# Fourier mixing and a squared-ReLU layer on one core: angle tables built by other engines in another order, weights loaded later, one small permutation of the second block moved

## The chip, the core and the metric

The kernel runs on one core of a Trainium2 chip. The core has a matrix engine (TensorE, PE in the profile; its weight loads are PEld), a vector engine (VectorE, DVE), a scalar engine (ScalarE, ACT), a general engine (GpSimd, POOL) and a synchronisation engine (SyncE, SP). Each works through its own list of instructions in order, and they meet only at semaphores. On-chip memory is SBUF, with 128 partitions; matrix products land in PSUM. POOL here also issues nearly all loads. A load issued by POOL occupies POOL while its descriptors are made, and is carried out by 16 DMA engines later.

The metric is device time in microseconds (us). Before the change it is 598.44 us, the median of three runs (597.36 to 598.6).

## The reference

`x` has shape (8, 3008, 256), `w_in` (256, 2048), `w_out` (2048, 256), all float32.

```python
X = np.fft.fft(x, axis=1)
X = np.fft.fft(X, axis=2)
x = X.real.reshape(B * S, D)
h = np.maximum(x @ w_in, 0.0)
return h * h @ w_out
```

## The kernel before

The 2-D transform's real part is written as cosine and sine products. The cosine and sine matrix over the 256 features is multiplied into `w_in` first, which gives `gh` (three float16 matrices of 128 rows and 2048 columns). The transform over 3008 rows is folded several times by symmetry, so that TensorE multiplies folded rows `od` by tables `cos_t` and `sin_t` of 376 columns. Results of all eight blocks (batches) are laid side by side in one long line of columns, which is cut into windows of 240, 512, 376, 376, 512, 448 and then 512 columns. For each window TensorE multiplies `gh` by the window's `zc` and `zs` (lines 859, 860, 882), ScalarE applies ReLU, VectorE squares (`power`, line 898), and one window later TensorE multiplies by `wout16` (line 704). The order of the work is written out by hand (`tc.manual_schedule()`): the order of the Python calls is the order on each engine.

What follows concerns the time before the first window and the second window (`w == 1`).

**Loads.** POOL issues, in this order, a direct load of half of the first block `x` (line 127), two gathers of the other half (line 132), two loads for `w16` (line 180, `w_in`), one for `wout16` (line 329), and later three loads of the second block. Loads of one queue land in their order of issue.

**Tables.** `table_steps(0)` makes the tables in two halves of three rows (h = 0, 1). The angle is frequency times row number, reduced modulo the period. `args` (ACT, line 232, three instructions for each half) makes `t`, a rounded number of turns; `turns` (line 238) scales it, on DVE for half 0 and on POOL for half 1; `mods(0)` (DVE, line 254, three instructions) multiplies the frequency `kf` by the row `nvec` and adds `t`. For half 1 the same is done in two steps: `kns(1)` (ACT, line 244, three instructions) makes the product `m`, `sums(1)` (DVE, line 248, one instruction of 1128 elements) adds `t`. `sins` (ACT, line 260) turns `m` into `sin_t`. `weigh` (POOL, line 281) halves one row of `sin_t` on one partition, with a weight `wgt` that POOL makes (lines 322, 323). `coss` (lines 270, 271) makes two rows of `cos_t` at a time: two TensorE products with a permutation matrix (`perm`, POOL, line 326) turn rows of `sin_t` over, and ACT copies them out of PSUM. The second `coss` reads the weighed row.

`s_n` and `c_all` (ACT, lines 315, 317, 331) are the feature tables, from `am` and `at` on DVE.

**First fold.** `u_half` and `u_odd` (DVE, lines 396, 400) subtract quarters of the first block, `u_part(0)` (lines 403, 370) gives `od`; a copy of one row (line 397) lies between the first two. `edge` (ACT, line 407) sets column 0 of `od`.

**TensorE's list before window 0.** 44 products on zeros (`idle`, line 307), `coss(0)`, 4 more on zeros, `coss(1)`, `coss(2)`, 5 more, then the first three products with `od` (line 581, `pz`), then `gh_step(0)`: four products of `c_all` and `s_n` with `w16` (line 527), then `nyq` (lines 453 to 455: two small products of `perm` with column d = 128 of `od`, and a DVE copy of the result into column 0 of the sine half of `od`), more of line 581, `gh_step(1)`, then the first products of window 0 (line 938). `gh_turn` (DVE, line 534) needs `turn2`, which POOL makes after its loads (lines 337, 338). After `gh_turn(1)` DVE adds the quarters of block zero (`v_even`, line 410), which frees `x` for the load of block one.

**Window 1** goes by pairs of steps, p = 0 to 3. In each, TensorE makes `pq(s0)` and `pq(s1)` (four products each), ACT applies ReLU to both. DVE folds block one meanwhile (lines 431, 442, 435, 445, and 448, which writes `od`). For p = 3 the calls are

```python
pq(s0); relu(s0, 0); pq(s1); relu(s1, 0)
run(*post[s0 - 1])          # nyq of block one
settle(); power(s1, 0, 1)   # the squares that wait
run(*zl)                    # 12 products pz with od
```

and at the end of p = 2 one square is taken out of turn: `kept.pop(0)()`.

Of the kernel before, what the change touches and what calls it, by code (L numbers as in the profile page):

```python
# [10 lines left out]
F16 = mybir.dt.float16  # L11
# [5 lines left out]
P = 128  # L17
# [12 lines left out]
def kernel(  # L30
# [145 lines left out]
    xs = {0: load_x(0, idx_first)}  # L176
    prow_i = iota([P, P], [[1, P]], 0, 1, "prow_i")
    w16 = [wp.tile([P, 2, F // 2], F16, name=f"w16_{i}", tag="w16") for i in range(2)]
    for i in range(2):
        nc.gpsimd.dma_start(out=w16[i], in_=moe_w_in[:, i * F // 2 : (i + 1) * F // 2].rearrange("(c p) f -> p c f", p=P))  # L180
# [26 lines left out]
    def table_steps(e):  # L207

        n = unit_cols[e][0]
        nr = 2 if e else 3  # L210
        cos_t = const.tile([P, 2 if e else R, n], F16, name=f"cos{e}")
        sin_t = const.tile([P, 2 if e else R, n], F16, name=f"sin{e}")
        tabs[e] = (cos_t, sin_t)
        vec, vs = (evec, evs) if e else (nvec, nvs)
        st = {}

        def row(h, j):
            return j if e else RQ[3 * h + j]

        def freq():  # L220
            kf = st["kf"] = tmp.tile([P, NE], F32, name="kf", tag="kf")[:, 0:n]
            i = 0
            for k0, kstep, cnt in unit_runs[e][0]:
                nc.vector.tensor_scalar(out=kf[:, i : i + cnt], in0=irow[:, i : i + cnt], scalar1=float(kstep), scalar2=float(k0 - kstep * i), op0=ALU.mult, op1=ALU.add)
                i += cnt

        def args(h):
            t = st["t", h] = tmp.tile([P, 3 * NE], F32, name="t", tag="tt").rearrange("p (j n) -> p j n", j=3)
            for j in range(nr):
                r = row(h, j)  # L230
                if e == 0:
                    nc.scalar.activation(t[:, j, 0:n], st["kf"], AF.Copy, bias=R23, scale=vs[:, r : r + 1])
                else:
                    nc.vector.tensor_scalar(out=t[:, j, 0:n], in0=st["kf"], scalar1=vs[:, r : r + 1], scalar2=R23, op0=ALU.mult, op1=ALU.add)

        def turns(h, eng=nc.vector):
            t = st["t", h]
            eng.tensor_scalar(out=t[:, 0:nr, 0:n], in0=t[:, 0:nr, 0:n], scalar1=-R23, scalar2=-float(S), op0=ALU.add, op1=ALU.mult)

        def kns(h):  # L240
            m = st["m", h] = tmp.tile([P, 3, NE], F32, name="m", tag="tm")
            for j in range(nr):
                r = row(h, j)
                nc.scalar.activation(m[:, j, 0:n], st["kf"], AF.Copy, bias=0.0, scale=vec[:, r : r + 1])

        def sums(h):
            m = st["m", h][:, 0:nr, 0:n]
            nc.vector.tensor_tensor(m, m, st["t", h][:, 0:nr, 0:n], op=ALU.add)

        def mods(h):  # L250
            m = st["m", h] = tmp.tile([P, 3, NE], F32, name="m", tag="tm")
            for j in range(nr):
                r = row(h, j)
                nc.vector.scalar_tensor_tensor(out=m[:, j, 0:n], in0=st["kf"], scalar=vec[:, r : r + 1], in1=st["t", h][:, j, 0:n], op0=ALU.mult, op1=ALU.add)

        def absm(h):
            nc.vector.tensor_scalar(out=st["t", h][:, 0:nr, 0:n].bitcast(I32), in0=st["m", h][:, 0:nr, 0:n].bitcast(I32), scalar1=0x7FFFFFFF, scalar2=None, op0=ALU.bitwise_and)

        def sins(h):
            nc.scalar.activation(sin_t[:, 3 * h : 3 * h + nr, :], st["m", h][:, 0:nr, 0:n], AF.Sin, bias=0.0, scale=wk)  # L260

        def coss(h):
            if e:
                nc.scalar.activation(cos_t, st["t", h][:, 0:nr, 0:n], AF.Sin, bias=halfpi[:, 0:1], scale=-wk)
                return

            pc = ps_h.tile([P, 2, 512], F32, name="pc", tag="psh")
            for j in range(2):
                r = RQ[2 * h + j]
                nc.tensor.matmul(pc[:, j, 0:n], perm[1 if r else 0], sin_t[:, RQ.index(6 - r if r else 0), :], start=True, stop=True)  # L270
            nc.scalar.activation(cos_t[:, 2 * h : 2 * h + 2, :], pc[:, :, 0:n], AF.Copy, bias=0.0, scale=1.0)

        def weigh():
            if e:
                for t in (cos_t, sin_t):
                    for r in range(2):
                        nc.vector.tensor_scalar(out=t[:, r, :], in0=t[:, r, :], scalar1=wge[:, r : r + 1], scalar2=None, op0=ALU.mult)
                return

            q = RQ.index(1)  # L280
            nc.gpsimd.tensor_scalar(out=sin_t[:, q, :], in0=sin_t[:, q, :], scalar1=wgt[:, 0:1], scalar2=1.0, op0=ALU.mult, op1=ALU.mult)
# [24 lines left out]
        for i in range(n):  # L306
            nc.tensor.matmul(pw[:, 0 : 3 * P], spn[:, 0, 0, :], spn.rearrange("p c r d -> p (c r d)")[:, 0 : 3 * P], start=True, stop=True)
# [16 lines left out]
    perm = [const.tile([P, P], F16, name=f"perm{i}") for i in range(2)]  # L324
    for i in (1, 0):
        nc.gpsimd.tensor_scalar(out=perm[i], in0=prow_i, scalar1=float(P - 1 - i), scalar2=None, op0=ALU.is_equal)
    to["sums"](1)

    nc.gpsimd.dma_start(out=wout16, in_=moe_w_out.rearrange("(c p) o -> p c o", p=P))
# [3 lines left out]
    pick = const.tile([P, 1], F16, name="pick")  # L333
    nc.gpsimd.memset(pick, 0.0)
    nc.gpsimd.memset(pick[0:1, :], -2.0)
    turn2 = small([P, 1], "turn2")
    nc.gpsimd.tensor_scalar(out=turn2, in0=dvec[:, 0:1], scalar1=0.0, scalar2=2.0, op0=ALU.is_equal, op1=ALU.mult)
    nc.gpsimd.tensor_scalar(out=turn2, in0=turn2, scalar1=-2.0, scalar2=None, op0=ALU.add)
    evec_i = iota([P, 2], [[1, 2]], 0, 2, "evec_i")
    idx["c"] = iota([P, 1], [[1, 1]], P - 1, -1, "idx_c")  # L340
    nc.gpsimd.memset(idx["c"][0:2, :], P - 3)
    idx["f"] = iota([P, 1], [[1, 1]], -1, 1, "idx_f")
    nc.gpsimd.memset(idx["f"][0:1, :], 0)
    evec = small([P, 2], "evec")
    nc.gpsimd.tensor_copy(evec, evec_i)
    evs = small([P, 2], "evs")
    nc.gpsimd.tensor_scalar(out=evs, in0=evec, scalar1=1.0 / S, scalar2=None, op0=ALU.mult)
    wge = small([P, 2], "wge")
    wg2 = small([P, 2], "wg2")
    nc.gpsimd.tensor_scalar(out=wge, in0=evec, scalar1=float(G), scalar2=0.5, op0=ALU.is_le, op1=ALU.mult)  # L350
    nc.gpsimd.tensor_scalar(out=wg2, in0=evec, scalar1=float(G), scalar2=0.5, op0=ALU.is_lt, op1=ALU.mult)
    nc.gpsimd.tensor_tensor(wge, wge, wg2, op=ALU.add)
    nc.gpsimd.tensor_scalar(out=wg2, in0=evec, scalar1=0.0, scalar2=-0.5, op0=ALU.is_equal, op1=ALU.mult)
    nc.gpsimd.tensor_tensor(wge, wge, wg2, op=ALU.add)
    to["sins"](1)
    folded = {}

    fe = fo = None
# [462 lines left out]
    for w in range(NW):  # L821
# [141 lines left out]
        elif w == 1:  # L963
            zl = [j for zu, part, h in zj for j in zu(part, h)]
            for p in range(NST // 2):
# [97 lines left out]
```

## Time and profile before

| what | us |
|---|---|
| median of three runs | 598.44 |
| the profiled execution's own time | 597.31 |
| its span, first to last instruction | 595.5 |
| TensorE busy (x4421) | 584.9 |
| VectorE busy | 497.0 |
| ScalarE busy | 462.2 |
| GpSimd busy | 243.9 |

The profiled execution is 1.13 us below the median, and 1.81 us of it lie outside the span. A line of the trace gives the start and the duration of an instruction or of several of one kind (x6), its engine, its line in the code, what it writes and reads, and in brackets how long the engine had been idle before it and whose end ended that. Starts are counted from the first instruction.

### The profile page before, as it was taken

The page shows a single profiled execution, that of the slowest core. Times are in us where ns is not written, and L with a number is a line of the kernel's source. Part 1 is how long each engine was busy: PE and PEld are TensorE (multiplying, and loading weights), DVE is VectorE, ACT ScalarE, POOL GpSimd, SP SyncE. Part 2 cuts the span into 40 slices and gives each one's busy share as a digit, 9 for nine tenths or more (in the row PEclk, how much of TensorE's full clock was granted, in tenths as well). Part 3 has the DMA queues.
Part 4 walks back from the last instruction along what each step waited for, and adds up shares of the span by engine and source line. Part 5 has one row for each costly group of instructions (what it writes and reads, how often), then busy time and mean ns, then how long its engine had stood idle before and what let it go on. Part 6 is the DMA issues. An engine that isn't in the chain of part 4 may idle for free.

```text
span 595.5 us, 11299 instructions
## 1 busy us (share of the span) xinstructions
PE 584.9 (98%) x4421; PEld 424.9 (71%) x4421; DVE 497.0 (83%) x582; ACT 462.2 (78%) x617; POOL 243.9 (41%) x304
## 2 busy tenths in 40 slices
PE   7999999999999999999999999999999999999997
PEld 4567786776776777777777777777777777777786
DVE  8988686987989778979899799979899799888871
ACT  6796777967797787788878788877877788788762
POOL 8411423166514506183253651446505724425310
PEclk9999999999999999999999999999999999999999
DMA  8946421137211461246123442145312321211212
GB/s 149 154 87 149 123 73 44 48 108 148 61 44 55 129 138 49 72 101 155 41 59 108 94 116 58 38 121 115 90 39 90 87 58 37 61 47 48 61 56 70
DMA packets 37624, 50.33 MB, mean 85 GB/s; under 512 B 4589, under 2 KB 30755, under 8 KB 37571
## 3 DMA queue, kind: packets, MB, share of 16 engines
q0 software_dynamic: 10400, 24.94, 20.6%
q1 hardware_dynamic: 26899, 24.44, 13.6%
q8 instruction: 34, 0.56, 0.4%
q10 hardware_dynamic: 272, 0.23, 0.1%
q14 instruction: 19, 0.16, 0.1%
HBM read 36.42 MB, written 27.86 MB: 108 GB/s over the span
## 4 chain that ended last, share of the span: by engine, by line
PE 81%; DVE 10%; ACT 3%; POOL 2%; issue 2%; DMA 1%; DVEq 0%; ACTq 0%; POOLq 0%
PE po L704 47%; PE ph L882 6%; PE ph L859 6%; PE ph L860 6%; PE ph L877 6%; PE ph L868 5%; PE pz L581 4%; DVE h L898 2%; DVE t L872 2%; DVE h L889 2%; DMA xo<-in_x_dram,idx_r 1%; ACT h L891 1%; DVE zc L610 1%; ACT h L902 1%; POOL xo L132 1%
## 5 line engine op out<-in xcount | busy, mean ns | idle before, releaser
L704 PE MATMUL po<-wout,h 128*128 128x256 f16 (+1 forms) x3024 | 364.8, 273 | 0.0
L704 PEld LDWEIGHTS <-h 128*128 128x128 f16 (+1 forms) x3024 | 296.8, 98 | 75.1
L891 ACT ACTIVATE h<-ph 128x1024 f16<-128x1024 f32 (+3 forms) x301 | 287.6, 991 | 64.2 <-PE ph L877 41.1
L898 DVE TENSOR_TENSOR h<-h 128x2048 f16<-128x2048 f16 (+7 forms) x199 | 189.9, 960 | 22.1 <-ACT h L891 18.9
L818 POOL TENSOR_SCALAR n<-zn,g2n 128x512 f32<-128x512 f16 (+3 forms) x166 | 156.2, 954 | 68.7 <-DMA zn<-rd 55.5
L872 DVE SCALAR_TENSOR_TENSOR t<-ph,n 128x1024 f32<-128x1024 f32 (+3 forms) x83 | 99.1, 1194 | 37.5 <-PE ph L868 32.1
L889 DVE CUSTOM_DVE_ANT_0 h<-t,ph 128x1024 f16<-128x1024 f32 x74 | 90.0, 1216 | 15.5 <-ACT h L891 15.1
L902 ACT ACTIVATE h<-h 128x1024 f16<-128x1024 f16 (+3 forms) x87 | 90.3, 1038 | 0.5
L719 ACT ACTIVATE osb<-po 128x512 f32<-128x512 f32 (+3 forms) x95 | 55.0, 584 | 37.0 <-PE po L704 32.5
L859 PE MATMUL ph<-zc,gh 128*128 128x512 f16 (+3 forms) x218 | 80.3, 369 | 0.4 <-ACT h L950 0.3
L860 PE MATMUL ph<-zs,gh 128*128 128x512 f16 (+3 forms) x218 | 80.2, 368 | 0.0
L810 POOL DMA_DIRECT2D zn<-rd x22 | 12.7, 579 | 161.9 <-DMA rd<-zs 153.6
L882 PE MATMUL ph<-zs,gh 128*128 128x512 f16 (+3 forms) x218 | 62.5, 368 | 0.3 <-ACT h L891 0.3
L877 PE MATMUL ph<-zs,gh 128*128 128x512 f16 (+3 forms) x166 | 48.4, 373 | 0.9 <-DVE t L872 0.4
L868 PE MATMUL ph<-zc,gh 128*128 128x512 f16 (+3 forms) x166 | 48.4, 373 | 0.0
L859 PEld LDWEIGHTS <-gh 128*128 128x128 f16 x218 | 21.2, 97 | 22.9 <-DVE h L889 1.6
L860 PEld LDWEIGHTS <-gh 128*128 128x128 f16 x218 | 21.3, 98 | 22.1 <-issue 0.9
L868 PEld LDWEIGHTS <-gh 128*128 128x128 f16 x166 | 16.2, 98 | 18.9 <-issue 0.5
L882 PEld LDWEIGHTS <-gh 128*128 128x128 f16 x218 | 20.2, 98 | 4.1 <-issue 0.7
L586 ACT ACTIVATE es<-pz 128x376 f32<-128x376 f32 (+1 forms) x32 | 14.8, 485 | 8.9 <-PE pz L581 8.7
L464 POOL DMA_DIRECT2D scr<-ev x8 | 4.7, 582 | 40.7 <-DVE ev L460 34.8
L132 POOL DMA_INDIRECT xo<-in_x_dram,idx_r x15 | 17.7, 1182 | 4.5 <-issue 4.3
(143 smaller groups left out, 368.2 us busy)
## 6 DMA issues: line engine op xcount, KB each, us to landing
out_dram<-osb SPq DMA_DIRECT2D x77, 128.0 KB
xo<-in_x_dram POOLq DMA_DIRECT2D x7, 768.0 KB, 6.8
scr<-ev POOLq DMA_DIRECT2D x8, 390.0 KB, 4.0
zn<-rd POOLq DMA_DIRECT2D x19, 128.0 KB, 3.9
rb<-scr POOLq DMA_DIRECT2D x16, 130.0 KB, 3.9
out_dram<-osb SPq DMA_DIRECT2D x12, 94.0 KB
w<-in_moe_w_in_dram POOLq DMA_DIRECT2D x2, 512.0 KB, 10.0
wout<-in_moe_w_out_dram POOLq DMA_DIRECT2D x1, 1024.0 KB, 11.0
```

The source lines that it names most:

```text
L704: nc.tensor.matmul(po[0:m, j * D : (j + 1) * D], h2[:, fc, q : q + m], wout16[:, fc, :], start=(fc == 0 and not both), stop=(fc == NFC - 1 ...
L818: nc.gpsimd.tensor_scalar(out=n2[:, a, 0:wn1], in0=zns[wt][:, 0:wn1], scalar1=g2n[:, fc : fc + 1], scalar2=1.0, op0=ALU.mult, op1=ALU.mult)
L859: nc.tensor.matmul(ph[:, a, 0:wn], gh[:, 0, f0 : f0 + P], zcw[:, 0:wn], start=True, stop=False)
L860: nc.tensor.matmul(ph[:, a, 0:wn], gh[:, 1, f0 : f0 + P], zsw[:, 0:wn], start=False, stop=True)
L868: nc.tensor.matmul(ph[:, a, 0:wn], gh[:, 0, f0 : f0 + P], zcw[:, 0:wn], start=True, stop=True)
L872: nc.vector.scalar_tensor_tensor(out=t2[:, :, 0:wn], in0=phs[s][:, :, 0:wn], scalar=-2.0, in1=n2s[w, s][:, :, 0:wn], op0=ALU.mult, op1=ALU ...
L877: nc.tensor.matmul(phs[s][:, a, 0:wn], gh[:, 1, f0 : f0 + P], zsw[:, 0:wn], start=False, stop=True, skip_group_check=True)
L882: nc.tensor.matmul(phs[s][:, a, 0:wn], gh[:, 2, f0 : f0 + P], zsw[:, 0:wn], start=False, stop=True, skip_group_check=True)
L889: nc.vector._custom_dve(TENSOR_ADD_SAT, out=h, in0=t2s[s][:, :, 0:wn], in1=phs[s][:, :, 0:wn], s0=BIG, s1=0.0)
L891: nc.scalar.activation(h, phs[s][:, :, 0:wn], AF.Relu, bias=0.0, scale=-1.0)
L898: nc.vector.tensor_tensor(h, h, h, op=ALU.mult)
L902: nc.scalar.activation(h, h, AF.Square, bias=0.0, scale=1.0)
```

## The change

Nothing that is computed changes. In the stretch before window 0:

- `kns(0)` is new: three ACT instructions make the angle product of half 0, and `mods(0)` on DVE (three instructions) gives way to `sums(0)` (one).
- `kns(1)` goes from ACT to POOL: three `tensor_scalar` of 376 elements.
- `weigh` goes from POOL to ACT, and its weight `wgt` (two instructions on one element) from POOL to DVE.
- POOL's list is now: the three loads of block zero, `prow_i`, `perm` twice, `kns(1)`, `turns(1)`, and only then the two loads of `w16` and the load of `wout16`, then `pick`, `turn2` and the small constants as before.
- ACT's list is now: `args(0)`, `kns(0)`, `args(1)`, `sins(0)`, `s_n`, `c_all`, the edge of `s_n`, `weigh`, `sins(1)`, and then all three `coss` copies, `edge`.
- DVE's list is now: `turns(0)`, `sums(0)`, `u_half` with its row copy, `wgt`, `sums(1)`, `u_odd`, `u_part(0)`. `sums(1)` waits for POOL alone.

In window 1, `nyq` of block one comes right after `pq(6)` instead of after `pq(7)`, and the square taken out of turn at the end of p = 2 goes back into its turn, behind `nyq`'s copy. TensorE has the same instructions as before in the same order, but for those two small products. SP's list is the same.

```diff
-    for i in range(2):
-        nc.gpsimd.dma_start(out=w16[i], in_=moe_w_in[:, i * F // 2 : (i + 1) * F // 2].rearrange("(c p) f -> p c f", p=P))
...
         def kns(h):
...
+                if h:
+                    nc.gpsimd.tensor_scalar(out=m[:, j, 0:n], in0=st["kf"], scalar1=vec[:, r : r + 1], scalar2=1.0, op0=ALU.mult, op1=ALU.mult)
+                    continue
                 nc.scalar.activation(m[:, j, 0:n], st["kf"], AF.Copy, bias=0.0, scale=vec[:, r : r + 1])
...
-            nc.gpsimd.tensor_scalar(out=sin_t[:, q, :], in0=sin_t[:, q, :], scalar1=wgt[:, 0:1], scalar2=1.0, op0=ALU.mult, op1=ALU.mult)
+            nc.scalar.activation(sin_t[:, q, :], sin_t[:, q, :], AF.Copy, bias=0.0, scale=wgt)
...
-    idle(44)
-    to["args"](0)
-    to["args"](1)
-    to["kns"](1)
-    nc.scalar.activation(s_n, am, AF.Sin, bias=0.0, scale=-wd)
-    nc.scalar.activation(c_all, at, AF.Sin, bias=halfpi[:, 0:1], scale=-wd)
-    to["turns"](0)
-    to["mods"](0)
-    to["turns"](1, nc.gpsimd)
-    nc.gpsimd.tensor_scalar(out=wgt, in0=nraw[:, 1:2], scalar1=float(Q), scalar2=-0.5, op0=ALU.is_equal, op1=ALU.mult)
-    nc.gpsimd.tensor_scalar(out=wgt, in0=wgt, scalar1=1.0, scalar2=None, op0=ALU.add)
-    for i in (1, 0):
-        nc.gpsimd.tensor_scalar(out=perm[i], in0=prow_i, scalar1=float(P - 1 - i), scalar2=None, op0=ALU.is_equal)
-    to["sums"](1)
-    nc.gpsimd.dma_start(out=wout16, in_=moe_w_out.rearrange("(c p) o -> p c o", p=P))
-    to["sins"](0)
-    nc.scalar.activation(s_n[:, :, 0:1], c_all[:, :, P : P + 1], AF.Copy, bias=0.0, scale=0.5)
-    to["weigh"]()
...
-    to["sins"](1)
...
     f0s = fold_steps(0)
     z0 = z_steps(need[0][0], late=True)
-    run(f0s["u_half"], f0s["u_odd"], lambda: f0s["u_part"](0))
+    idle(44)
+    to["args"](0)
+    to["kns"](0)
+    to["args"](1)
+    for i in (1, 0):
+        nc.gpsimd.tensor_scalar(out=perm[i], in0=prow_i, scalar1=float(P - 1 - i), scalar2=None, op0=ALU.is_equal)
+    to["kns"](1)
+    to["turns"](0)
+    to["sums"](0)
+    to["turns"](1, nc.gpsimd)
+    for i in range(2):
+        nc.gpsimd.dma_start(out=w16[i], in_=moe_w_in[:, i * F // 2 : (i + 1) * F // 2].rearrange("(c p) f -> p c f", p=P))
+    nc.gpsimd.dma_start(out=wout16, in_=moe_w_out.rearrange("(c p) o -> p c o", p=P))
+    to["sins"](0)
+    nc.scalar.activation(s_n, am, AF.Sin, bias=0.0, scale=-wd)
+    nc.scalar.activation(c_all, at, AF.Sin, bias=halfpi[:, 0:1], scale=-wd)
+    nc.scalar.activation(s_n[:, :, 0:1], c_all[:, :, P : P + 1], AF.Copy, bias=0.0, scale=0.5)
+    f0s["u_half"]()
+    nc.vector.tensor_scalar(out=wgt, in0=nraw[:, 1:2], scalar1=float(Q), scalar2=-0.5, op0=ALU.is_equal, op1=ALU.mult)
+    nc.vector.tensor_scalar(out=wgt, in0=wgt, scalar1=1.0, scalar2=None, op0=ALU.add)
+    to["weigh"]()
+    to["sums"](1)
+    to["sins"](1)
...
+    run(f0s["u_odd"], lambda: f0s["u_part"](0))
     to["coss"](0)
     idle(4)
     to["coss"](1)
...
                 pq(s0)
                 if p < 2:
                     settle()
+                elif s1 == NST - 1:
+                    run(*post[s0 - 1])
                 relu(s0, 0)
                 pq(s1)
                 relu(s1, 0)
                 if s1 == NST - 1:
-                    run(*post[s0 - 1])
                     settle()
...
                 run(*at[s0], *at[s1], *f2q[2 * n :])
-                if p == 2:
-                    kept.pop(0)()
```

More of the change, by code (lines that the diff above doesn't have):

```diff
@@ L307, in idle @@
             nc.tensor.matmul(pw[:, 0 : 3 * P], spn[:, 0, 0, :], spn.rearrange("p c r d -> p (c r d)")[:, 0 : 3 * P], start=True, stop=True)
-    idle(44)
-    to["args"](0)
-    to["args"](1)
-    to["kns"](1)
+    perm = [const.tile([P, P], F16, name=f"perm{i}") for i in range(2)]
     wd = 2.0 * math.pi / D
     s_n = const.tile([P, 2, P + 1], F16, name="s_n")
-    nc.scalar.activation(s_n, am, AF.Sin, bias=0.0, scale=-wd)
     c_all = const.tile([P, 2, P + 1], F16, name="c_all")
-    nc.scalar.activation(c_all, at, AF.Sin, bias=halfpi[:, 0:1], scale=-wd)
@@ L329 @@
-    nc.gpsimd.dma_start(out=wout16, in_=moe_w_out.rearrange("(c p) o -> p c o", p=P))
-    to["sins"](0)
-    nc.scalar.activation(s_n[:, :, 0:1], c_all[:, :, P : P + 1], AF.Copy, bias=0.0, scale=0.5)
-    to["weigh"]()
[L333 to L354, printed above, removed]
-    to["sins"](1)
     folded = {}
@@ new lines @@
+    to["weigh"]()
+    to["sums"](1)
+    to["sins"](1)
+    pick = const.tile([P, 1], F16, name="pick")
+    nc.gpsimd.memset(pick, 0.0)
+    nc.gpsimd.memset(pick[0:1, :], -2.0)
+    turn2 = small([P, 1], "turn2")
+    nc.gpsimd.tensor_scalar(out=turn2, in0=dvec[:, 0:1], scalar1=0.0, scalar2=2.0, op0=ALU.is_equal, op1=ALU.mult)
+    nc.gpsimd.tensor_scalar(out=turn2, in0=turn2, scalar1=-2.0, scalar2=None, op0=ALU.add)
+    evec_i = iota([P, 2], [[1, 2]], 0, 2, "evec_i")
+    idx["c"] = iota([P, 1], [[1, 1]], P - 1, -1, "idx_c")
@@ new lines @@
+    nc.gpsimd.memset(idx["c"][0:2, :], P - 3)
+    idx["f"] = iota([P, 1], [[1, 1]], -1, 1, "idx_f")
+    nc.gpsimd.memset(idx["f"][0:1, :], 0)
+    evec = small([P, 2], "evec")
+    nc.gpsimd.tensor_copy(evec, evec_i)
+    evs = small([P, 2], "evs")
+    nc.gpsimd.tensor_scalar(out=evs, in0=evec, scalar1=1.0 / S, scalar2=None, op0=ALU.mult)
+    wge = small([P, 2], "wge")
+    wg2 = small([P, 2], "wg2")
+    nc.gpsimd.tensor_scalar(out=wge, in0=evec, scalar1=float(G), scalar2=0.5, op0=ALU.is_le, op1=ALU.mult)
@@ L647 @@
+    nc.gpsimd.tensor_scalar(out=wg2, in0=evec, scalar1=float(G), scalar2=0.5, op0=ALU.is_lt, op1=ALU.mult)
+    nc.gpsimd.tensor_tensor(wge, wge, wg2, op=ALU.add)
+    nc.gpsimd.tensor_scalar(out=wg2, in0=evec, scalar1=0.0, scalar2=-0.5, op0=ALU.is_equal, op1=ALU.mult)
+    nc.gpsimd.tensor_tensor(wge, wge, wg2, op=ALU.add)
+    run(f0s["u_odd"], lambda: f0s["u_part"](0))
     to["coss"](0)
```

1 line of the change is left out of this document (removed).

## The prediction, made before the changed kernel was run

> **What bounds the kernel now.** I read the page's head first, then TensorE's waits, then the chain of waits over the first 62 us, then the rows of single tiles.
>
> ```profile
> span 595.5 us, 11299 instructions
> PE 584.9 (98%) x4421; PEld 424.9 (71%) x4421; DVE 497.0 (83%) x582; ACT 462.2 (78%) x617; POOL 243.9 (41%) x304
> ```
>
> TensorE is busy for 98% of the span. By stage, 549.1 us from 46.4 us on hold 543.8 us of TensorE work, so this change, which ends at about 46 us, can only move the start of that block. Its waits, longest first, say where:
>
> ```profile
> PE pc L270 <- POOL pick L334: 2.0, 1, 2.0
> PE pw L307 <- DVE spn L189: 1.2, 1, 1.2
> PE pz L581 <- ACT od L407: 0.6, 1, 0.6
> PE ph L944 <- ACT h L950: 0.5, 2, 0.3
> PE pz L581 <- DVE od L455: 0.5, 1, 0.5
> ```
>
> The first is `coss(1)` waiting for `weigh` (shown as `pick`, POOL's next instruction), the third the wait before the first `pz`, the fifth `nyq` of block one. The chain gives both places:
>
> ```profile
> 9.66 1.65 POOL perm L326 x2
> 11.31 0.39 issue
> 11.71 1.23 POOL wout L329
> 12.94 0.09 issue
> 13.03 1.36 POOL sin L281
> 14.39 0.05 POOL pick L334
> 14.44 0.49 PE pc L270 x2
> 14.94 0.02 issue
> 14.96 1.49 ACT cos L271 x2
> 16.45 0.13 ACT od L407
> 16.57 0.05 issue
> 16.62 0.65 PE pz L581 x3
> ...
> 43.87 0.19 DVE od L455
> 44.06 0.05 issue
> 44.10 0.67 PE pz L581 x3
> ```
>
> The reader is to see that the first `pz` at 16.62 hangs on POOL's list (`perm`, `wout16`, `weigh`), and that in window 1 `pz` follows DVE's copy at 43.87. The chain's `issue` before that copy is DVE in the square taken out of turn (42.73 to 43.95 in the timeline).
>
> How POOL and DVE hinder each other:
>
> ```profile
> L254 DVE SCALAR_TENSOR_TENSOR m<-kf,nvec,t x3: 598/600/1551, 7.4 to 9.4; 128x376 f32<-128x376 f32 x3
> L238 POOL TENSOR_SCALAR t<-t x1: 1139/1139/1139, 7.4 to 7.4; 128x1128 f32<-128x1128 f32 x1
> ```
>
> One of three equal DVE instructions took 1.55 instead of 0.60: it ran beside POOL's `turns(1)` of 1128 elements. That is 0.95 lost, 0.84 ns an element. The other way, POOL's second `perm` starts at 10.42 and takes 1.34 because DVE's sum runs until 11.36. So each waits for the other's instruction and they take turns.
>
> **The change part by part.** Times are of the profiled execution (597.31, span 595.5).
>
> *POOL's list.* A product of 376 elements on POOL takes 0.57 undisturbed (fastest `n<-zn` of 376 columns), and holds DVE for 376 x 0.84 ns = 0.32. `perm` (128 elements) then needs about 0.11 + 0.25 = 0.36. `prow_i` ends at 5.93 as before. `perm` one runs to 6.35. `turns(0)` starts at 6.33 as before; it took 1.07 beside the loads of `w16`, and 0.75 is my estimate without them (`kf`, the same form with 376 elements, takes 0.35). It ends at 7.08, `perm` two at 7.5. `sums(0)` waits for `kns(0)` on ACT (the sixth instruction of line 232's kind ends at 7.15), runs 7.2 to 8.6 (1.41, the sum's row), and the first product waits for it: 8.6 to 9.15. `u_half` (0.96) then runs 8.9 to 9.85, the second product to 10.4, the third to 10.95; the row copy (0.21 undisturbed; its gather lands at 3.32 + 6.9 = 10.2) and `wgt` (0.17 each, DVE's row for `nvs`) lie beside them. `turns(1)` (1.14) ends at 12.1; `args(1)` on ACT has ended at 8.7 and costs nothing. POOL without any turn lost would end at 9.85 (8.7 + 1.14); one turn more lost, at 12.6 to 12.9. I take 12.1, because every DVE instruction in this stretch but `wgt` is of the kind that made POOL wait above.
>
> *Tables.* `sums(1)` now waits for POOL only: 12.15 to 13.55 (before: 9.94 to 11.36). Behind it on DVE stand `u_odd`, two instructions of `u_part(0)`: 0.96 + 0.96 + 0.57, done by 16.1, in time. Behind it on ACT stand `sins(1)` and three copies, then `edge`, at the starts of the rows before: 1.05 + 3 x 0.70 + 0.23 = 3.4. So `pz` starts at 13.6 + 3.4 = 17.0 instead of 16.62: +0.4. What was gained at `weigh` (POOL 13.03 to 14.39; on ACT about 0.6, the row of line 232, between `wgt` at 11.3 and `sins(1)`, hidden) is given back, since `coss(0)`, which before ran at 12.44 under the wait, now stands behind `sins(1)`. `sins(0)`, some 1.4 earlier, gains nothing: its `coss(0)` products stand behind `idle(44)`, which ends at 11.3. Taking two DVE instructions out of `mods(0)` is hidden for the same reason.
>
> The Trainium skill (SBUF — State Buffer, "🔬 SBUF: two separate sides") says that VectorE and GpSimd share a port pair as an exclusive lock which the winner keeps for its whole instruction. The sums beside `perm` lost only 0.08 (1.04 against 0.96 for the two `u`), less than `perm`'s own time; with the whole 0.57 for each product instead of 0.32, three products would add 0.75 and the change would come to +1.6 instead of the sum below.
>
> *Weights.* The first load of `w16` is issued at 12.1 instead of 5.84, and the DMA queues stand empty from 12.06 (4.69 + 7.4, the last gather).
>
> ```profile
> L180 POOL DMA_DIRECT2D w<-in_moe_w_in_dram x2: 779/780/780, 5.8 to 6.6; - x2
> DMA to landing us min/median/max: 9.1/10.0/10.8
> ```
>
> Before, it landed at 5.84 + 9.1 = 14.9 and the second at 6.59 + 10.8 = 17.4, so one takes 2.45 to move. From an empty queue the block loads landed 7.1 and 6.7 after issue; two gathers of half that size land 1.8 apart, so the head costs 3.0 to 3.4, and `w16` lands 5.45 to 5.85 after issue: 17.55 to 17.95. `gh_step(0)` stands 0.49 behind `pz`, at 17.5: TensorE waits 0.05 to 0.45, I take 0.3. Queued behind this wait on TensorE are `nyq`, the sine half, `gh_step(1)` and window 0, so it counts in full. The second half lands at 20.2, before its use at 22.2 + 0.7. `wout16` lands 5.3 later, 25.5 (needed at 30.4), and block one's load, issued at 23.5 + 0.7, moves data only 2.5 after issue (DMA share 0.27 from 22.5 to 26.0, 1.03 after), so it isn't pushed. POOL's small constants follow at about 15.2 (three issues, 0.78 + 0.78 + 1.23); `turn2` needs 1.5, done by 16.8, before `gh_turn(0)` at 19.6. SP's queue is idle then.
>
> *Window 1.* `nyq`'s products stood at 43.44, now behind `pq(6)`, ready at 42.58; `od` is done at 42.82. TensorE waits 0.3 (to 42.88), and `pq(7)` ends 0.36 later than before (two products of 0.03 with it). The copy, no longer behind the square, is done at 43.3, so `pz` starts at 43.80, not 44.10: −0.3. But ReLU of `pq(7)` on ACT then starts at 44.0 instead of 43.75, and `es` behind it ends at 45.45 instead of 45.28, for which the third group of `pz` waits (45.33 before): +0.15. The gain of the first is lost in the second. Bounds −0.3 and +0.3 (the whole wait for `od`); I take +0.15, the later place. The square, now last of four, ends 0.4 later; the next results that DVE makes there (line 610) belong to window 3, and DVE has 0.53 idle at 49.5, so it costs nothing; without that cover 0.4.
>
> Sum: +0.4 + 0.3 + 0.15 = +0.85: 598.2 for the profiled execution, which stands 1.13 below the median, so 599.3 for the median.
>
> **The rivals.**
> - *POOL loses one more turn* (`perm` two also waits out `sums(0)`): `turns(1)` ends at 12.6 to 12.9, everything at the start 0.5 to 0.8 later, and `wout16` lands after 26, pushing block one by 0.3, which `nyq`'s wait passes on: +1.65 to +2.0, 600.2. For it: POOL's mean for 512 columns is 0.97 against 0.69 undisturbed.
> - *Faster: POOL keeps ahead of DVE.* `turns(1)` ends at 9.85; `sums(1)` then waits only for `u_half` and the row copy (10.2 + 0.2 + `wgt` 0.35), 10.85 to 12.25, `pz` at 15.7 (−0.9), `w16` at 15.5, before 16.2, and with the lower bound of window 1, −1.2: 597.2. It decides the sign as soon as `turns(1)` ends before 11.4. Against it: the two `perm` rows.
> - *No effect:* `w16` lands in time and `nyq` gains what the tables lose: 598.4 ± 0.3.
> - *TensorE's clock.* The first matmuls stand 0.32 apart until 6.6 us, later ones 0.16. If the idle stretch before `coss(1)` (12.4 to 14.44; by my sum to 14.75) grows so long that this returns, `gh_step(0)` and window 0 run at half pace for up to 5.4 us (1.22 to 6.6): about +2, 600.4. Against it: after 2.0 us idle the pace was still 0.16. The Trainium skill (TensorE: Matmul & The Clock Gate, "🔬 Part 1: The HAM clock gate (the "warmup" mystery)") puts the limit at an idle window of about 3.4 us; no run here shows it yet.
>
> **How the numbers follow.** Chances: my forecast 0.47, POOL one turn later 0.21, faster 0.18, no effect 0.09, clock 0.05. 0.2%, about what a measurement of this kernel can tell from no change, is 1.2 us. My forecast's own range is +0.1 to +1.6 (−0.3 in window 1 to 0.45 at `w16` and the lock held longer); a third of it, 0.16, lies beyond +1.2. Slower: 0.16 + 0.21 + 0.05 = 0.42. Faster: 0.13 of the 0.18. Within: 0.45. The range leaves out the far ends of the faster case and of the slow ones: 597.4 to 600.7.
>
> **What would show it.** Right: `turns(1)` on POOL ending near 12, `w16` issued right after, the four products of line 527 waiting for the DMA, `pc` waiting for ACT and not for POOL, `py` waiting for DVE's `od` at block one, and the third `pz` group there for `es`. Wrong: `pz` before 16.6 with `w16` landed (the faster case), matmuls 0.32 apart after 14 us (the clock), or any new wait of TensorE after 50 us, where I have costed the later square at nothing.

## The result, and the profile after

The changed kernel takes 600.02 us (median of 7, 599.51 to 601.55); the kernel before, run beside it, 597.72 (median of 7, 597.33 to 598.6). The ratio is 1.0042, 95% interval 1.0031 to 1.0054: 2.3 us slower, where +0.85 was forecast. The profiled execution took 599.94, with a span 2.6 us longer than before's.

The single times of either kernel lie in two groups by TensorE's granted clock (before, over all comparisons: 597.2 to 597.8 at 0.998 to 1.0 and 598.1 to 598.9 at 0.995 to 0.997; after: 599.5 to 600.0 at 0.997 to 0.999 and 601.3 to 601.6 at 0.994). Both medians of this comparison lie in the lower group; the one that the forecast was added to, 598.44, lay in before's upper one. Four single executions far outside (682.1 to 3511.56, two of them of the kernel before) enter no ratio below.

The page's head and first rows of the kernel after:

```profile
span 598.1 us, 11297 instructions
PE 585.9 (98%) x4421; PEld 424.9 (71%) x4421; DVE 496.4 (83%) x582; ACT 462.7 (77%) x618; POOL 243.3 (41%) x304
```

TensorE has 1.0 us more of busy time with the same 4421 matmuls, which already says that some of them ran at a lower pace. Its waits (line <- engine and line waited for: us in total, times, longest; `...` stands for rows left out):

```profile
PE pc L271 <- ACT sin L261: 2.5, 1, 2.5
...
PE pc L271 <- ACT sin L282: 0.7, 1, 0.7
PE pz L539 <- ACT es L544: 0.5, 1, 0.5
...
PE pg L485 <- DMA w<-in_moe_w_in_dram: 0.3, 1, 0.3
...
PE py L411 <- DVE od L406: 0.3, 1, 0.3
```

The 2.0 us wait for `weigh` on POOL is gone. In its place TensorE waits 2.5 us for `sins(1)`, then for `w16`. The rows with `es` and with `od L406` are window 1. The chain of waits (start us, us, what) shows which of these sets the time:

```profile
7.51 3.53 POOL m L243 x3
11.04 0.08 issue
11.12 1.13 POOL t L236
12.31 6.78 DMA w<-in_moe_w_in_dram
19.13 1.04 PE pg L485 x4
...
46.13 0.97 PE pz L539 x6
47.10 0.47 ACT es L544
47.62 1.12 PE pz L539 x6
```

Not the tables: the path runs through POOL's three products, `turns(1)`, and then 6.78 us of the first `w16` load. The 0.3 us that TensorE waits for it is no measure of its cost, because products at half pace stand ahead of it. The timeline of TensorE (start us, us, engine, line, operation, count, idle before) and the table by stretches (bounds and length, then the busy time of PE, PEld, DVE, ACT and POOL, then the clock, the DMA share and GB/s) show the pace. First the first `gh_step` of the kernel before, then the changed kernel:

```profile
17.11 0.59 PE L527 MATMUL pg<-w,c_all 128*128 128x512 f16 x2
```

```profile
16.11 1.80 PE L308 MATMUL pw<-spn 128*128 128x384 f16 x5
17.71 1.12 PE L539 MATMUL pz<-cos,od 128*128 128x376 f16 x3
19.13 0.61 PE L485 MATMUL pg<-w,c_all 128*128 128x512 f16 x2 [0.30 <-DMA w<-in_moe_w_in_dram]
20.06 0.64 PE L539 MATMUL pz<-cos,od 128*128 128x376 f16 x3
```

```profile
12.00:17.00 5.00, 2.11 (x7) 0.88 (x7) 4.61 (x6) 3.16 (x4) 4.66 (x14) 0.83 0.60 69
17.00:22.00 5.00, 4.70 (x23) 2.08 (x22) 2.19 (x5) 1.78 (x6) 1.65 (x6) 0.83 1.13 185
```

Three `pz` products take 1.12 at 17.71 and 0.64 at 20.06, and the clock is 0.83 in both stretches, where before it was 1.00. The trace's clock record holds half of full speed (0.5) from 15.26 to 18.67, that is for 3.41 us.

Laying the two traces over each other, the same TensorE instruction starts later than before by 1.10 us at the first `pz` (17.71 against 16.62), by 2.02 at the first `gh_step` (19.13 against 17.11), by 2.3 from the third `pz` group of window 1 on (47.62 against 45.33), and by 2.6 from 429 us, where one round trip of `zn<-rd` came 0.28 later. That last place is not touched by the change; what moved it is open.

### The profile page after: what moved, and what is told of

Same layout as the page of the kernel before. It is cut to its first block, busy times and chain, and to the rows that moved or that the text cites. A ratio compares the mean times of both kernels' runs of the same rounds, so it can differ in the third digit from the quotient of the medians.

```text
span 598.1 us, 11297 instructions
## 1 busy us (share of the span) xinstructions
PE 585.9 (98%) x4421; PEld 424.9 (71%) x4421; DVE 496.4 (83%) x582; ACT 462.7 (77%) x618; POOL 243.3 (41%) x304
## 4 chain that ended last, share of the span: by engine, by line
PE 79%; DVE 9%; DMA 4%; ACT 3%; issue 2%; POOL 1%; ACTq 0%; POOLq 0%; DVEq 0%
PE po L707 46%; PE ph L885 6%; PE ph L862 6%; PE ph L863 6%; PE ph L880 6%; PE ph L871 5%; PE pz L539 4%; DVE h L901 2%; DVE t L875 2%; ACT h L894 2%; DMA xo<-in_x_dram,idx_r 1%; DVE h L892 1%; DMA w<-in_moe_w_in_dram 1%; DMA rd<-zs 1%; DMA zn<-rd 1%
## 5 line engine op out<-in xcount | busy, mean ns | idle before, releaser
L432 POOL DMA_INDIRECT rb<-scr,idx_r x16 | 17.9, 1117 | 4.9 <-issue 4.9
```

## The experiments

Every ratio is to the kernel before, run in the same comparison. Three theories about the 2 us at `gh_step` stood against each other: the late `w16` load binds; TensorE's half pace binds; or the late tables bind, with POOL's products as the cause of either.

**The clock.** More products on zeros keep TensorE busy through its wait.

```diff
-    idle(4)
+    idle(24)
```

> The changed kernel with 24 instead of 4 products on zeros between the first and the second coss, so that TensorE has no idle stretch there. Three theories of the +2.3 us. Weights: the first gh_step waits for the first load of w16 (issued 12.3, landed 19.1), whatever the clock does; then the clock stays whole, the first pz stands at about 17.3, TensorE waits about 1.3 for the load instead of 0.3, gh_step stays at 19.1, and the time is within 0.3 of the changed kernel's lower executions (599.7), but its executions at 601.3 are gone, since those have one more stretch of half clock (0.994 against 0.997). Clock: half pace between 15.3 and 18.7 is the cost; gh_step at about 17.8, 1.3 faster, 598.4. Tables: no change.

Measured: 599.91, ratio 1.0045 (1.003 to 1.006). The profiled execution ran at full clock, and TensorE's timeline is

```profile
17.57 0.65 PE L539 MATMUL pz<-cos,od 128*128 128x376 f16 x3 [0.56 <-ACT od L365]
19.57 0.61 PE L485 MATMUL pg<-w,c_all 128*128 128x512 f16 x2 [1.34 <-DMA w<-in_moe_w_in_dram]
```

`pz` now takes 0.65, and TensorE waits 1.34 for `w16` instead. The 2 us remain at full clock: the half pace of the changed kernel's profiled execution was hidden under the load, and the load binds. It landed 7.2 after its issue here, so that `gh_step` stands at 19.57, 0.4 later than in the changed kernel. One thing did not come as expected: two of the six executions still took 601.2 and 601.4, at clock 0.997. The longer group is not removed by these zeros; TensorE still idles 1.34 ahead of `gh_step`.

**`kns(1)` back on ScalarE**, the rest of the change kept.

```diff
-                if h:
-                    nc.gpsimd.tensor_scalar(out=m[:, j, 0:n], in0=st["kf"], scalar1=vec[:, r : r + 1], scalar2=1.0, op0=ALU.mult, op1=ALU.mult)
-                    continue
                 nc.scalar.activation(m[:, j, 0:n], st["kf"], AF.Copy, bias=0.0, scale=vec[:, r : r + 1])
```

> The changed kernel with kns(1) back on ACT, all else as changed. POOL's list then ends turns(1) at about 10 instead of 12.25. Weights: w16 is issued at about 10, before the gathers have all landed (12.06), lands at about 15.5 to 16, and the start moves with the later of it and the tables: first pz about 15.9, gh_step about 16.5, 2.6 less than the changed kernel, 597.4 (a little under the kernel before, but for the 0.25 of window 1). Clock: nothing but half pace goes, about 0.4 to 1.3 less. If it were POOL's and DVE's taking turns on the tables alone, w16 would still land at 19 and nothing would change.

Measured: 597.62, ratio 1.0001 (0.9992 to 1.001). POOL's timeline:

```profile
8.72 1.13 POOL L236 TENSOR_SCALAR t<-t 128x1128 f32<-128x1128 f32 x1 [1.32 <-ACT t L230]
9.91 1.55 POOL L612 DMA_DIRECT2D w<-in_moe_w_in_dram  x2
```

and TensorE's first `gh_step`:

```profile
17.16 0.60 PE L482 MATMUL pg<-w,c_all 128*128 128x512 f16 x2 [0.63 <-DMA w<-in_moe_w_in_dram]
```

`turns(1)` starts 2.4 earlier, the loads are issued 2.4 earlier (9.91 against 12.31), and the first `gh_step` is back at 17.16. The whole cost against the kernel before is gone with these three instructions. I had expected the load at 15.5 to 16; it landed at 17.12, 7.2 after its issue, and still held `gh_step` by 0.63. So the load itself takes longer than I had priced it. Five of the eleven executions took 598.0 to 598.8 with the clock at 0.999 to 1.0; what lengthened these is not known, and it is not the clock.

**Window 1 put back** in the changed kernel, and **window 1 alone** in the kernel before.

```diff
                 pq(s0)
-                elif s1 == NST - 1:
-                    run(*post[s0 - 1])
...
                 if s1 == NST - 1:
+                    run(*post[s0 - 1])
...
+                if p == 2:
+                    kept.pop(0)()
```

> The changed kernel with window 1 as before: nyq of block one behind pq(7), the square out of turn again. My theory (later place: es behind ReLU of pq(7)): 0.25 faster than the changed kernel, third pz group of block one 2.04 later than in the kernel before instead of 2.30. Rival: the move gains the 0.3 of the first pz group and undoing it costs up to 0.2.

> The kernel before with the window-1 part of the change alone (nyq of block one behind pq(6), the square back in its turn). My step: the first pz group of block one 0.3 earlier, the third 0.15 later (it waits for es, which stands behind ReLU of pq(7)), 0.15 to 0.25 slower in all (598.0 beside 597.8). Rival from the changed kernel's numbers: the move costs nothing (the interval holds 1), since TensorE is even elsewhere in the window.

Measured: put back, 1.0039 (1.0024 to 1.0054), single times 599.5 to 599.7 at clock 0.996 to 0.997 and 601.1 to 601.3 at 0.994, like the changed kernel's own; alone, 597.96, 0.9999 (0.999 to 1.0007). The chain of window 1, of the kernel with window 1 alone:

```profile
42.76 0.16 PE py L453
...
43.84 0.97 PE pz L581 x6
44.81 0.47 ACT es L586
45.28 0.04 issue
45.33 1.11 PE pz L581 x6
```

By the timeline `pz` starts at 43.68 instead of 44.10 (the chain counts it from the end of the instruction ahead), `es` still ends at 45.28, and the third group still starts at 45.33, to the hundredth where it stood before. No effect of this part shows in the times either way; the intervals would hide one of up to 0.6.

**`weigh` alone on ScalarE**, in the kernel before.

```diff
-            nc.gpsimd.tensor_scalar(out=sin_t[:, q, :], in0=sin_t[:, q, :], scalar1=wgt[:, 0:1], scalar2=1.0, op0=ALU.mult, op1=ALU.mult)
+            nc.scalar.activation(sin_t[:, q, :], sin_t[:, q, :], AF.Copy, bias=0.0, scale=wgt)
```

> The kernel before with one part of the change alone: weigh on ACT instead of POOL. w16 stays early (lands 14.9). coss(1) no longer waits for POOL; first pz at 15.4 to 15.8 instead of 16.62, bounded by od on DVE and by ACT's list; 0.8 to 1.2 faster than the kernel before, about 596.7. Rival: w16, DVE or the clock takes the place of the wait, and the gain is under 0.3.

Measured: 596.53, ratio 0.9979 (0.997 to 0.9988). TensorE's waits:

```profile
PE pz L581 <- DVE od L455: 0.8, 1, 0.8
PE pz L581 <- DVE od L370: 0.7, 1, 0.7
```

This is the good part of the change, and it stands 1.1 below the kernel with `kns(1)` back on ScalarE (597.62), in which the load, issued at 9.91 instead of 5.86, takes most of this gain away again: it holds `gh_step` by 0.63 there. The first `pz` comes at 15.69 and `gh_step` at 16.16, 0.95 earlier than before; `pz` now waits for VectorE's first fold (second row), and 0.4 is lost in window 1, where the copy of `nyq` is later relative to the products (first row).

**The late loads alone**: the kernel before with `weigh` on ScalarE, as in the last edit, and besides that the two `w16` loads moved from behind `prow_i` to behind `perm`.

```diff
-    for i in range(2):
-        nc.gpsimd.dma_start(out=w16[i], in_=moe_w_in[:, i * F // 2 : (i + 1) * F // 2].rearrange("(c p) f -> p c f", p=P))
...
     for i in (1, 0):
         nc.gpsimd.tensor_scalar(out=perm[i], in0=prow_i, scalar1=float(P - 1 - i), scalar2=None, op0=ALU.is_equal)
+    for i in range(2):
+        nc.gpsimd.dma_start(out=w16[i], in_=moe_w_in[:, i * F // 2 : (i + 1) * F // 2].rearrange("(c p) f -> p c f", p=P))
```

> The kernel with weigh on ACT, and the two loads of w16 issued behind perm instead of ahead of turns(1), so issued at about 10.5 instead of 5.86. Tables as in the run with weigh on ACT alone (first pz about 15.7, perhaps a little earlier, since POOL has 1.5 less ahead of them). Weights: the load lands 6.8 to 7.2 after issue, at about 17.5, gh_step(0) waits for it (16.16 without), so 1.3 to 1.6 slower than weigh on ACT alone: 597.9. Tables or clock: no slower than weigh on ACT alone, 596.5.

Measured: 600.34, ratio 1.0035 (1.0023 to 1.0047). TensorE's timeline:

```profile
15.06 0.64 PE L581 MATMUL pz<-cos,od 128*128 128x376 f16 x3 [0.25 <-ACT od L407]
18.66 1.03 PE L527 MATMUL pg<-w,c_all 128*128 128x512 f16 x2 [2.96 <-DMA w<-in_moe_w_in_dram]
19.49 1.06 PE L527 MATMUL pg<-w,s_n 128*128 128x512 f16 x2
```

With tables that are early (`pz` at 15.06) the load issued at 11.49 lands at 18.62, 7.1 later; TensorE waits 2.96 and its clock falls (1.03 for two products instead of 0.6). The one execution at clock 1.0 took 598.95, 2.4 more than the 596.53 of the kernel with `weigh` alone; the others took 1.2 to 2.4 on top. A late load is enough to lose the gain of `weigh` and more, and it cost more than the 1.3 to 1.6 that I had expected, since POOL reached its issue 1.0 later than I had put it.

**The early loads alone**: the changed kernel, with the `w16` loads issued where they were before the change.

```diff
     prow_i = iota([P, P], [[1, P]], 0, 1, "prow_i")
+    for i in range(2):
+        nc.gpsimd.dma_start(out=w16[i], in_=moe_w_in[:, i * F // 2 : (i + 1) * F // 2].rearrange("(c p) f -> p c f", p=P))
...
     to["turns"](1, nc.gpsimd)
-    for i in range(2):
-        nc.gpsimd.dma_start(out=w16[i], in_=moe_w_in[:, i * F // 2 : (i + 1) * F // 2].rearrange("(c p) f -> p c f", p=P))
```

> The changed kernel with the two loads of w16 issued where they were before (ahead of perm). They land at about 15 and 17.5. POOL's perm, kns(1) and turns(1) stand 1.5 later. Weights alone were the cost: gh_step at 16.2 to 17.3, 2 faster, 598. Weights and tables both (my sum): turns(1) ends at about 13.5, sums(1) at about 14.9, first pz at 18.4, gh_step at 18.9 or later: within 0.5 of the changed kernel, since the tables then take the place of the weights.

Measured: 600.11, ratio 1.003 (1.0018 to 1.0042). POOL's timeline, and TensorE's:

```profile
7.65 2.22 POOL L611 TENSOR_SCALAR perm<-prow_i 128x128 f16<-128x128 int32 x2
9.96 1.70 POOL L245 TENSOR_SCALAR m<-kf,nvec 128x376 f32<-128x376 f32 x3
11.75 1.13 POOL L238 TENSOR_SCALAR t<-t 128x1128 f32<-128x1128 f32 x1
```

```profile
15.47 0.47 PE L273 MATMUL pc<-sin,perm 128*128 128x376 f16 x1 [3.60 <-ACT sin L263]
18.34 1.14 PE L541 MATMUL pz<-cos,od 128*128 128x376 f16 x3
19.28 1.06 PE L487 MATMUL pg<-w,c_all 128*128 128x512 f16 x2
```

Now `w16` lands at 14.88, but POOL's list is no shorter: `turns(1)` ends at 12.88 (12.25 in the changed kernel), TensorE idles 3.60 in one stretch, and its clock is at half from 14.24 to 21.07. `gh_step` stands at 19.28, where it had been with the late load (19.13). So the late loads are not the only limit: with `kns(1)` on POOL either the tables or the loads are late, whichever goes last. How much of this kernel's cost is the tables themselves and how much the half pace that their wait brings is not separated: the clock fell in all six executions (0.993 to 0.997). In the trace `edge` ends at 17.90, 1.3 later than before, and the rest of the 2.2 at `gh_step` is products at half pace.

**Why the load takes 6.8.** Three tries: the `wout16` load issued only after the small constants (at 19.06); a small load of two columns of `w_in` by SP at the start, read by nobody, to take a first access out of the way; and the second `w16` load and `wout16` both held back to 18.2.

```diff
     for i in range(2):
         nc.gpsimd.dma_start(out=w16[i], in_=moe_w_in[:, i * F // 2 : (i + 1) * F // 2].rearrange("(c p) f -> p c f", p=P))
-    nc.gpsimd.dma_start(out=wout16, in_=moe_w_out.rearrange("(c p) o -> p c o", p=P))
...
     nc.gpsimd.tensor_tensor(wge, wge, wg2, op=ALU.add)
+    nc.gpsimd.dma_start(out=wout16, in_=moe_w_out.rearrange("(c p) o -> p c o", p=P))
```

> The changed kernel with the load of wout16 issued behind POOL's small constants (about 18 instead of 13.8). In the changed kernel the first load of w16 took 6.8 from issue, 4.6 of it moving at some 60% of the pace that its second half has, and wout16 was being issued meanwhile. Theory wout: its descriptors slow the load; the load then lands at about 17.7 (5.4 after issue) and gh_step moves to the end of the pz group, about 18.2 to 18.7: 0.4 to 0.9 faster than the changed kernel. Rival: the pace is that of a load that starts on an empty queue; it lands at 19.1 and nothing changes, or wout16 comes late for window 1.

```diff
+    seen = const.tile([P, 2, 2], F32, name="seen")
+    nc.sync.dma_start(out=seen, in_=moe_w_in[:, 0:2].rearrange("(c p) f -> p c f", p=P))
```

> The changed kernel with one small load more, on SP's queue at the start: two columns of every row of w_in, which nothing reads. In the changed kernel the first load of w16 moved at 60% of the pace of the second. Theory first access: the first read of these rows is slow and the small load pays for it; then the load lands at about 17.8, gh_step follows the pz group at about 18.4 to 18.7, 0.4 to 0.7 faster. Rival, empty queue: the pace is that of a load of this shape that starts when nothing is queued; it lands at 19.1 and the time is the changed kernel's, 600.0.

```diff
-    for i in range(2):
-        nc.gpsimd.dma_start(out=w16[i], in_=moe_w_in[:, i * F // 2 : (i + 1) * F // 2].rearrange("(c p) f -> p c f", p=P))
-    nc.gpsimd.dma_start(out=wout16, in_=moe_w_out.rearrange("(c p) o -> p c o", p=P))
+    nc.gpsimd.dma_start(out=w16[0], in_=moe_w_in[:, 0 : F // 2].rearrange("(c p) f -> p c f", p=P))
...
     nc.gpsimd.tensor_tensor(wge, wge, wg2, op=ALU.add)
+    nc.gpsimd.dma_start(out=w16[1], in_=moe_w_in[:, F // 2 : F].rearrange("(c p) f -> p c f", p=P))
+    nc.gpsimd.dma_start(out=wout16, in_=moe_w_out.rearrange("(c p) o -> p c o", p=P))
```

> The changed kernel with the second load of w16 (and that of wout16) issued only behind the small constants, some 4.5 us after the first (12.3), so that the first load has the queues to itself until about 17. If the slow pace of the first load comes from the second load's descriptors being made beside it, the first lands 5.45 to 5.85 after its issue, near 18, and the first gh_step starts near 18.0. If a load of this form simply takes that long from an empty queue, it lands 6.8 to 7.2 after issue, near 19.1 to 19.5, as before. Either way the second half comes later than its use at 24 or so, so the time as a whole is no better: 600 to 602; only the first landing decides.

Measured: 599.99, 1.0033 (1.0021 to 1.0045), the first load landing 6.96 after its issue; 601.79, 1.0053 (1.0038 to 1.0067), 6.96; 603.17, 1.0084 (1.0053 to 1.0115), 5.96. The last kernel's POOL and TensorE timelines:

```profile
12.06 0.80 POOL L614 DMA_DIRECT2D w<-in_moe_w_in_dram  x1
18.20 0.81 POOL L647 DMA_DIRECT2D w<-in_moe_w_in_dram  x1
19.01 1.18 POOL L648 DMA_DIRECT2D wout<-in_moe_w_out_dram  x1
```

```profile
18.19 0.59 PE L485 MATMUL pg<-w,c_all 128*128 128x512 f16 x2
25.09 0.59 PE L485 MATMUL pg<-w,c_all 128*128 128x512 f16 x2 [1.68 <-DMA w<-in_moe_w_in_dram]
```

Neither `wout16` nor a first access is the cause. Alone in the queue the first load lands 5.96 after its issue (18.02), and `gh_step` no longer waits for it; it stands at 18.19 all the same, held by the tables at half pace. The second half, issued at 18.20 with `wout16` right behind it, again takes 6.85 (25.05). So, by this one trace against seven, the load takes 0.8 to 1.2 longer when another is issued right behind it. The packets show where the time goes: alone, its data moves for 4.19 us, and it lands 0.28 after its last packet; in the changed kernel they are 4.64 and 0.64. The other half's first packet starts at 18.27 there, when the first half's last one is about to end (18.45), so the two do not share the engines while the first moves. Why the first is slower then stays open. The whole time is worse here because the second half comes too late for its use (TensorE waits 1.68), and because the rows of block one, queued behind it, land 11.83 after their issue instead of 8.10, for which TensorE waits 2.2 in window 1.

**The clock in the kernel before.** Zeros through its 2.0 us wait.

```diff
-    idle(4)
+    idle(17)
```

> The kernel before with 17 instead of 4 products on zeros in the 2.0 us in which TensorE waits for weigh. In 8 of 23 executions of the kernel before beside the first experiments, and 11 of 19 beside the second, the clock was 0.996 and the time about 1.0 longer. Clock theory: these executions are gone, all are at 597.2 to 597.8. Rival: the clock falls for another reason and they stay.

Measured: 597.42 (597.31 to 597.52, 11 executions), ratio 0.9989 (0.998 to 0.9998), the clock 0.999 or 1.0 in all of them. The kernel before beside it had 12 of 17 executions at 0.995 to 0.997, near 598.3. These are gone:

```profile
11.62 2.93 PE L307 MATMUL pw<-spn 128*128 128x384 f16 x17
14.44 0.80 PE L270 MATMUL pc<-sin,perm 128*128 128x376 f16 x4
```

The tables are ready at 14.44 as before, with no idle ahead. The gap of 2.0 us had let the clock fall in most of these executions, at about 1.0 us each. With `weigh` alone on ScalarE, where that gap is gone too, ten executions stand at 0.998 to 1.0.

**A version that beats both**: the kernel before with `weigh` on ScalarE, the row copy of `u_half` ahead of its subtraction (so that the first fold ends earlier), and no square taken out of turn in window 1.

```diff
-            nc.gpsimd.tensor_scalar(out=sin_t[:, q, :], in0=sin_t[:, q, :], scalar1=wgt[:, 0:1], scalar2=1.0, op0=ALU.mult, op1=ALU.mult)
+            nc.scalar.activation(sin_t[:, q, :], sin_t[:, q, :], AF.Copy, bias=0.0, scale=wgt)
...
         def u_half():
+            nc.vector.tensor_copy(t[0:1, 2, 0, :], t[0:1, 0, R - 1, :])
             nc.vector.tensor_tensor(u[:, 0], t[:, 0], t[:, 1], op=ALU.subtract)
-            nc.vector.tensor_copy(t[0:1, 2, 0, :], t[0:1, 0, R - 1, :])
...
-                if p == 2:
-                    kept.pop(0)()
```

> The kernel with weigh on ACT alone, and two more edits: the row copy ahead of u_half's subtraction on DVE (it then runs before wout16 is issued, which held it for 0.48), and no square out of turn in window 1 (nyq's copy then isn't behind it; in the run with weigh on ACT TensorE waited 0.85 for that copy). od on DVE at about 15.1, first pz at 15.2, gh_step at 15.7 with w16 landed at 15.1: 0.45 less than weigh on ACT alone, and 0.3 to 0.5 less in window 1: 595.7. Rival: es behind ReLU bounds window 1 and only the 0.45 comes: 596.1.

Measured: 595.92 (595.89 to 596.44, 5 executions), ratio 0.9966 (0.9953 to 0.9979). TensorE's timeline:

```profile
15.24 0.65 PE L581 MATMUL pz<-cos,od 128*128 128x376 f16 x3 [0.21 <-ACT od L407]
15.72 0.59 PE L527 MATMUL pg<-w,c_all 128*128 128x512 f16 x2
```

`gh_step` stands 1.39 earlier than before, no gap of TensorE between 9 us and there exceeds 0.5 us, the clock stands at 0.999 to 1.0 in all five executions, and window 1 is 20.06 long (20.24 before, 20.62 with `weigh` alone). Some 0.5 of this is lost after window 1: the last matmul comes 1.06 earlier than in the kernel before. Of the 2.3 between the medians some 0.8 is the clock, as the experiment ahead of this one prices it.

## Why the prediction was right and wrong

The forecast was 599.3; 600.02 lies 0.7 above it, inside the range of 597.4 to 600.7. That it lies inside is partly luck. The difference, +2.3, is beyond the forecast's own range of +0.1 to +1.6; it was added to a median, 598.44, that two of its three executions had put in the upper group, 0.7 above the one measured beside the changed kernel, and 598.44 + 2.3 would have been 600.7, at the very end of the range. The direction and the mechanism held: what `weigh` frees is given back by POOL's longer list and by the later weights. The size did not.

- *POOL's list: right.* `turns(1)` ended at 12.25, forecast 12.1. The rival of one more turn (12.6 to 12.9) and that of POOL keeping ahead (9.85) both fell. The three products took 1.73, 1.26 and 0.57, the last one undisturbed at exactly the price taken. The Trainium skill's rule (SBUF — State Buffer, "🔬 SBUF: two separate sides") that the winner holds the shared port for its whole instruction, from which I had worked out 0.75 more, is not borne out in that size by these products: `u_half`, which began beside the first of them, took 1.18, that is 0.22 over the undisturbed 0.96. Beside a longer instruction it nearly is: with `kns(1)` back on ScalarE, `u_half` ran beside `turns(1)` (1.13) and took 1.89, 0.93 over.
- *Tables: the term was small, +0.4, and would have been +0.7.* `sums(1)` ran 12.29 to 13.62 (forecast 12.15 to 13.55), but `edge` ended at 17.28 instead of 17.0, since ScalarE's last `coss` copy waited 0.18 for products at half pace. The five products on zeros behind them, at 0.32 apart, put `pz` at 17.71. All of this lies under the load and cost nothing.
- *Weights: this is the step that failed.* I had the load at 5.45 to 5.85 after its issue, from a head of 3.0 to 3.4 and 2.45 to move. It took 6.78, and 7.0 to 7.2 in the six other traces that issued it late with the other half behind it. The term was +0.7 at `gh_step` (0.4 of it the tables) and measured +2.02. The head came from the block's loads and the 2.45 from the distance of two landings in a queue that was already full; added together they price a load that has the queues to itself (5.96 measured), not one with another issued right behind it. The nearest row of the trace of before said so: the block's loads, each with gathers behind it, landed 6.7 and 7.1 after issue, and I took the head from them but not the whole.
- *Window 1: the term was +0.15, and the part alone moved the third group by 0.00.* As forecast, `py` waits for `od` and the gain at `pz` is lost behind `es`; I had `es` at 45.45 behind a later ReLU; alone it ended at 45.28, as before. In the changed kernel 0.25 is lost there all the same, with `od` 0.14 later after the start of the window; putting the part back did not shorten the executions, though in its trace the third `pz` group comes 16.52 after the window's first product, against 16.92 in the changed kernel and 16.68 before.
- *The clock: the mechanism of this rival is real, its price was another.* It had 0.05 and +2. The pace fell in six of seven executions of the changed kernel. Where it fell for one window of 3.41 us it cost nothing, because TensorE would have waited for `w16` anyway (the one execution in which it did not fall took 600.02). Where it fell for two windows, the time is 601.3 to 601.6 instead of 599.5 to 600.0: 1.5. My argument against it, that the pace was still 0.16 after 2.0 us of idling, held for the profiled execution alone; in 31 of the 59 executions of the kernel before beside the first eleven experiments the clock did fall.
- *A wait after 50 us* was named as something that would make it wrong; none came from the later square.

## What to carry to other kernels

Before a product moves to an engine that also issues loads, count what it does to the time of issue, and price a load from an empty queue by a whole row of its own kind, with another load behind it if there will be one, not by parts added together. Keep early loads ahead of arithmetic on such an engine: issued at 11.49 instead of 5.86, they alone cost 2.4 us (598.95 against 596.53, both at full clock). Keep the arithmetic off it too, if tables wait for it: with the three products on POOL, early loads did not help. Look at TensorE's granted clock over many executions, and try products on zeros in a wait of 2 us: they took 0.8 us off the median of the kernel before at no cost, and next to nothing off that of the changed kernel, where the load set the time.

## What the runs showed of the hardware that I had not expected

- *The clock falls after a window that is mostly idle, not only after an empty one.* In the trace's clock record every fall comes a whole number of windows of 3.413 us after the clock first rose (from 5.02 to 15.26 in the changed kernel is three), and lasts one or two of them. In the window before each of the eight falls that came ahead of a kernel's end TensorE worked for 0.3 to 1.6 us of 3.41 (0.64 in the changed kernel, 1.44 in the kernel with `weigh` and late loads); around gaps after which it did not fall, for 1.5 to 2.2 (2.0 in the kernel before and in the one with `kns(1)` back, 1.48 with window 1 alone). The two overlap, so busy time alone does not settle the bound. By the number of products begun in the window the same traces do not overlap: 1 to 8 ahead of a fall, 9 or more where there was none. A fall lasted a second window where TensorE worked 2.0 to 2.25 us in the first one (five traces), and ended after one where it worked 3.1 or more (the changed kernel, and twice with the loads apart). The Trainium skill (TensorE: Matmul & The Clock Gate, "🔬 Part 1: The HAM clock gate (the "warmup" mystery)") has the same 3413 ns and a window that runs freely; that agrees with the record here, and it would explain (this is argued, not shown) why the same 2.0 us gap costs 1.0 us in some executions and nothing in others. Its idle window of about 3.4 us, taken as the shortest gap that matters, does not agree: gaps of 2.0 and 2.5 were enough.
- *A load from an empty queue landed later when another was issued right behind it*: 5.96 us alone (one trace), 6.78 to 7.2 with another, of one form and size, although the other moved no data until the first was nearly through. The Trainium skill (DMA: Bandwidth & Descriptors, "🔬 Anatomy of one DMA — SWDGE (gpsimd) path") has a fixed 2.0 us and 436 GB/s, which for the 1 MiB that this load reads is an estimate of 4.4 us; the shortest that this load took here is 5.96.
